# The A11 B11 product of a gated MLP's gate and up as a second Strassen level, with a new order of instructions in a pair's first block

## The chip, the cores and the metric

The kernel runs on one core of one Trainium2 chip. The metric is the device time of one execution in microseconds; a profiled execution also gives the span, from the first to the last instruction of the program.

## The reference, cut to what matters

```python
x = A_x                                              # 1 x 2048 x 640, fp32
g = sigmoid((x * gate_w).sum(-1, keepdims=True))
a = Re(DFT_seq(DFT_hid(x)))                          # einsums with 640x640 and 2048x2048 matrices
b = (gelu(x @ w_gate) * (x @ w_up)) @ w_down         # 640 -> 1728 -> 640
return g * a + (1 - g) * b
```

All arrays are fp32.

## The kernel before, in words

Every fp32 product is made of three fp32r matmuls (`mm3`, L95): an operand is split into `high`, a copy in fp32r by ScalarE, and `low`, the rest, by VectorE; then high x high, high x low and low x high are added up in PSUM. One such triple, 128 x 128 weights on 512 columns, is "a product" here.

The work runs in stages. First, block 0 of the hidden dimension F and the odd 64 columns are computed as plain products. Then comes the loop `for f in range(1, NF)` over 12 blocks of 128 hidden columns (gate and up). After that W_down (`step_k`, 28 steps in `kseq`), then the sequence DFT (`cseq`, 64 steps), then the hidden DFT (`useq`). x and the weights are cut in 2 x 2 block matrices, and all large products use Winograd's form of Strassen's algorithm: seven block products named A11, A12, S1, S2, S3, S4 and A22 in place of eight, with sums T1 to T4 of x's blocks and S1 to S4 of the weights'. Gate is one row of the block matrix and up the other: the first half of the 640 inputs against the second, halves of 1024 rows of x against each other (tp 0 and 1), and a fifth group of 128 inputs by itself (g5, u5 and D).

Blocks 1 and 2 of F are done alone (kind 0). Blocks 3 to 12 are done in five pairs (3,4), (5,6) to (11,12): kind 1 is the pair's first block, kind 2 its second. In a pair, the A12 product of gate (`together`) and the A22 T4 product of up (`together_up`) of both blocks and both halves of x are done with a second Strassen level, 7 products in place of 8. The A11 B11 product isn't: `gate_up` computes it in each block for each half, two products each, and adds the result in PSUM (X) to S2 T2, and from PSUM to the tiles s1 that lead to the gate. The second levels need sums of sums: of x (`xp`, `xv`, made once by `sums_across`, kept in device memory and loaded again in every pair as `xq` and `xu` by `load_across`, three parts of 512 KB each, on POOL's queue), and of weights (`wq` in `make_w`, `wu` in `make_up`).

The order inside a block is written by hand: generators (`gate_up`, `together`, `together_up`) yield after each group of matmuls, and `run` puts ahead of a group's follow-up what `fill` takes from the list `fills`: sums and splits of the next weights, each with a cost in units of 10 ns, paced so that a block's share of fills keeps up with its share of TensorE time. `in_order` fixes the program's order on PE, ACT, DVE and POOL in this stage; SP's loads were ordered by the scheduler of the framework. A tile's buffers come from a pool `s4` of 46 slots of 512 KB, 32 of which x's blocks hold in this stage, and from 14 buffers of 256 KB (`m`): a load waits until its buffer's last reader is done. PSUM has 8 banks.

From the second pair on, the lows of `wa` and `wq` of a first block are not made by VectorE: ScalarE writes the negated high (`negative`), and an accumulating DMA on POOL's queue adds the raw weights (`left_of`).

The gate g is made along the way: `load_z` loads 128 rows of x, one DVE instruction multiplies them with gate_w and sums up (a "z row", 16 in all); `gates` takes the Sigmoid in block 12, `gate_rows` turns the result with a TensorE transpose and stores g and 1 - g, and `gate_tile` loads them spread over all partitions.

Of the kernel before, what the change touches and what calls it, by code (L numbers as in the profile page):

```python
# [15 lines left out]
P = 128  # L16
# [4 lines left out]
NS = S // P  # L21
NP = NS // 2
# [3 lines left out]
XN_AT = [1, 5, 16, 24]  # L26
GM_AT = [2, 15]
EORD = [0, 2, 1, 3, 4]
PAIRED = 3
Z_AT = [5, 10]  # L30
# [4 lines left out]
def kernel(  # L35
# [52 lines left out]
    def negative(lo, raw):  # L88

        nc.scalar.activation(lo, raw, AF.Copy, scale=-1.0)  # L90

    def left_of(lo, raw):

        nc.gpsimd.dma_start(lo, raw, accum_op=ALU.add)

# [23 lines left out]
    ident = pool.tile([P, P], F32, tag="ident", name="ident")  # L119
    z = pool.tile([P, NS], F32, tag="z", name="z")  # L120
# [7 lines left out]
    grd, gmd = (dram.tile([1, S], F32, tag=n, name=n) for n in ("grd", "gmd"))  # L128
# [80 lines left out]
    def load_w(f):  # L209


        if f >= NF:
            return
        ra, rb = slot(F32, [P, 8, P], f"wa{f}r"), wsmall(F32, f"wb{f}")
        nc.sync.dma_start(ra, wf[f - 1, :, :8])
        nc.sync.dma_start(rb, wf[f - 1, :, 8:])
        rq = None
        if pair_of(f) == 1:
            rq = slot(F32, [P, 8, P], f"wq{f}r")
            nc.sync.dma_start(rq[:, 0:2], wf[f, :, 0:2])  # L220
            nc.sync.dma_start(rq[:, 2], wf[f, :, 4])
        wraw[f] = ra, rb, rq

    def load_up(f):

        r = slot(F32, [P, 8, P], f"wu{f}r")
        nc.sync.dma_start(r[:, 0:2], wf[f, :, 2:4])
        nc.sync.dma_start(r[:, 6:8], wf[f - 1, :, 2:4])
        return r

    late_work = []

    def make_up(f, r):

        W, own = {}, {}
# [7 lines left out]
        def high_u():  # L243
            own["u"] = [slot(F32R, [P, 8, P], f"wu{f}{n}") for n in "hl"]
            high(own["u"][0][:, 1:6], r[:, 1:6])
# [8 lines left out]
        return W, [(112, across), (0, high_u), (78, low_u)]  # L254

    def make_w(f):


        ra, rb, rq = wraw.pop(f)
# [17 lines left out]
        def across():  # L277
            tt(rq[:, 3], rq[:, 0], rq[:, 1], op=ALU.add)
            tt(rq[:, 5], ra[:, 0], rq[:, 0], op=ALU.subtract)
            tt(rq[:, 4], rq[:, 3], ra[:, 0], op=ALU.subtract)  # L280

        def across2():
            tt(rq[:, 6], ra[:, 1], rq[:, 4], op=ALU.subtract)
            tt(rq[:, 7], g5, rq[:, 2], op=ALU.subtract)

        def diff():
            d = wsmall(F32R, f"wd{f}")
            tt(rb[:, 1], g5, u5, op=ALU.subtract)
            split(d[:, 0], d[:, 1], rb[:, 1])
            W["D"] = d[:, 0], d[:, 1]  # L290
# [4 lines left out]
        def high_a():  # L295
            if kind == 2:
                v = slot(F32R, [P, 8, P], f"wa{f}")
                own["a"] = v[:, 0:4], v[:, 4:8]
                high(own["a"][0], ra[:, 4:])
            else:  # L300
                own["a"] = parts("wa")
                high(own["a"][0], ra)

        def low_a():
            a = own["a"]
            if kind == 2:
                low(*a, ra[:, 4:])
                W["D"], W["u5"] = at(a, 0), at(a, 3)
                for i in range(2):
                    W["A11", i] = at(a, 1 + i)  # L310
                return
            if kind == 1 and f > PAIRED:
                left_of(a[1], ra)
            else:
                low(*a, ra)
# [3 lines left out]

        def neg_a():  # L320
            negative(own["a"][1], ra)

        def high_q():
            own["q"] = parts("wq")
            high(own["q"][0][:, 1:], rq[:, 1:])

        def neg_q():
            negative(own["q"][1][:, 1:], rq[:, 1:])

        def low_q():  # L330
            q = own["q"]
            if f > PAIRED:
                left_of(q[1][:, 1:], rq[:, 1:])
            else:
                low(q[0][:, 1:], q[1][:, 1:], rq[:, 1:])
            W["A22p"], W["g5n"], W["Dp"] = at(q, 1), at(q, 2), at(q, 7)
            for k in range(4):
                W[f"S{k + 1}p"] = at(q, 3 + k)
# [12 lines left out]
        if kind == 1:  # L351
            if f > PAIRED:
                work = [(0, high_a), (0, neg_a), (84, across), (0, low_a), (56, across2), (0, high_q), (0, neg_q)]
                work += [(84, sums), (0, low_q), (84, sums2), (0, high_c), (56, diff), (122, low_c)]
            else:
                work = [(84, across), (56, across2), (0, high_a), (0, high_q), (122, low_a), (109, low_q)]
                work += [(84, sums), (84, sums2), (56, diff)]
                late_work.extend([(0, high_c), (122, low_c)])
        elif kind == 2:
            work = [(84, sums), (28, diff_here), (0, high_a), (84, sums2), (122, low_a), (61, high_c), (0, low_c)]  # L360
        else:
            work = [(84, sums), (0, high_a), (84, sums2), (0, high_c), (122, low_a), (56, diff), (122, low_c)]
# [49 lines left out]
    def together(f, W, Tp, s1, xs):  # L412


# [7 lines left out]
        mm3(Z, W["S1p"], Tp["T1"], True, False)  # L422
        mm3(Z, W["g5n"], x1[1], False, True)
# [6 lines left out]
        s1[0, 0] = copy(V, f"s1{f}00")  # L430
        yield
        mm3(H, W["S2p"], Tp["T2"], False, True)
# [3 lines left out]
        mm3(H, W["S3p"], Tp["T3"], False, True)  # L436
# [3 lines left out]
        mm3(Z, W["S4p"], Tp["B22"], False, False)  # L440
        mm3(Z, W["Dp"], x1[1], False, True)
        yield 136
        tt(s1[0, 1], s1[0, 1], Z, op=ALU.add)
        tt(s1[0, 1], s1[0, 1], xs[1], op=ALU.add)
        yield
        mm3(H, W["A22p"], Tp["T4"], False, False)
        mm3(H, W["g5n"], x1[0], False, True)
# [37 lines left out]
    def gate_up(f, W, B, tp, s5, s1t, xs, s4):  # L485
# [6 lines left out]
        X, Z = bank(f"pX{n}"), bank(f"pZ{n}")  # L492
        xs[tp] = X
# [7 lines left out]
        prod(X, "A11", (1, 1), True)  # L501
        yield 136
        if not kind:
            V = bank(f"pV{n}")
            nc.scalar.activation(V, X, AF.Copy)
        else:
            s1 = s1t[kind - 1, tp] if (kind, tp) != (1, 1) else None
            if s1 is not None:
                tt(s1, s1, X, op=ALU.add)
        yield  # L510
# [11 lines left out]
        yield  # L522
        prod(X, "S2", "T2", False)
# [3 lines left out]
        mm3(Z, W["D"], x2, False, False)  # L527
        yield 68
        if kind:
            s1 = s1t[kind - 1, tp]  # L530
            nc.scalar.activation(s1, s1, AF.Gelu_apprx_tanh)
        yield
# [7 lines left out]
        nc.scalar.activation(s2, s2, AF.Gelu_apprx_tanh)  # L540
        yield
        if not kind:
# [85 lines left out]
    def gates():  # L628
        nc.scalar.activation(z, z, AF.Sigmoid)
        nc.scalar.activation(table, table, AF.Gelu_apprx_tanh)  # L630

    def gate_rows():

        ps = bank("pgr")
        nc.tensor.transpose(ps[:NS, :P], z, ident)
        g = mtile(F32, "gr")
        nc.scalar.activation(g[:NS, :P], ps[:NS, :P], AF.Copy)
        nc.vector.tensor_scalar(g[:NS, P : 2 * P], g[:NS, :P], -1.0, 1.0, op0=ALU.mult, op1=ALU.add)
        for k, to in enumerate((grd, gmd)):
            nc.gpsimd.dma_start(to.rearrange("o (s p) -> (o s) p", p=P), g[:NS, k * P : (k + 1) * P])  # L640

    def gate_tile(row, tp, name):

        g = pair(F32, name)
        nc.sync.dma_start(g.rearrange("p t c -> p (t c)"), row[:, 2 * tp * T : 2 * (tp + 1) * T].to_broadcast([P, 2 * T]))
# [4 lines left out]
    def load_z(n):  # L650

        r, work = {}, []

        def load():
            sb = zq.pop(0)
            r[0] = sb, slot(F32, [P, D], f"xz{sb}")
            nc.sync.dma_start(r[0][1], xz[sb])
# [270 lines left out]
    make_identity(nc, ident)  # L928
# [91 lines left out]
    Tp, Tu = {}, {}  # L1020

    def sums_across(n, to, blocks, last):
# [19 lines left out]
        def part(k, src):  # L1042
            def do():
                if k == 3:
# [19 lines left out]
    def load_across(f, n, to, kept, k):  # L1064
        v = slot(F32R, [P, 2, T], f"{n}{f}{k}")
        nc.gpsimd.dma_start(v.bitcast(F32), kept[k - 1])
# [4 lines left out]
    def fill(ns):  # L1071

        state["pe"] += ns
        some = False
        while fills and not (some and not fills[0][0]) and state["done"] <= 1.25 * state["all"] * state["pe"] / state["pe_all"]:
            cost, do = fills.popleft()
            do()
            some = True
            state["done"] += cost

    def run(steps):

        ns = next(steps, None)
        if ns is not None:
            fill(ns)
            next(steps)

    s1t, s4 = {}, {}
    Tp.update(B11=at(Bs[0][2, 1], 0), B21=at(Bs[0][2, 1], 1), B22=at(Bs[1][2, 1], 1))
    blocks = [("11", xt[0, 2]), ("12", xt[2, 2]), ("22", xt[2, 3]), ("21", xt[0, 3])]  # L1090
# [3 lines left out]
    with in_order(PE, ACT, DVE, POOL):  # L1094
        for f in range(1, NF):
            kind = pair_of(f)
            if f == PAIRED:
                loadu()
                fills.extend([*t4, *u123[:3], *late_work, *u123[3:], *u4])
            fills.extend(todo)  # L1100
            todo.clear()
            if kind == 1:
                up, work = make_up(f, load_up(f))
                fills.extend(work)
            if kind == 1:
                lw, *w = sum_wd((f - PAIRED) // 2)
                lw[1]()
                fills.extend(w)
            if f == PAIRED - 1:
                loadp()  # L1110
                fills.extend(t123)
            if f == NF - 1:
# [457 lines left out]
```

## Time and profile before

| what | value |
|---|---|
| runs, us | 1022.82, 1023.52, 1023.52; median 1023.52 |
| the profiled execution | 1023.77 us, span 1022.0 us |
| granted TensorE clock | 1.0 |
| HBM | read 186.19 MB, written 68.17 MB, 249 GB/s over the span |
| the loop over f = 1 to 12 | about 46 to 334.5 us of the span |

A row of a timeline gives start and duration in us, engine (PE matmul, PEld weight load, DVE VectorE, ACT ScalarE, POOL GpSimd, SPq a queue of DMA issues), line of the kernel, operation, tiles written and read, shape, and in brackets how long the engine was idle before and what ended that. A row of groups has a count, the busy time, the mean duration in ns and the idle time before. A row of DMAs has the count, the size of one and the median time from issue to landing. Matmul rows overlap, since matmuls are pipelined.

### The profile page before, as it was taken

What the parts mean: (1) busy time and instruction counts of PE and PEld (TensorE: products, weight loads), DVE (VectorE), ACT (ScalarE), POOL (GpSimd) and SP (SyncE); (2) the same over time, 40 slices, a digit from 0 to 9 for tenths busy, and PEclk for the clock granted to TensorE, in tenths of its full rate; (3) what the DMA queues carried; (4) which work ended last, traced back from release to release, by engine and by line L of the source; (5) the groups of instructions that cost most, each with busy time, mean ns of one, the idle gap of its engine ahead of it and who ended that gap; (6) DMA issues with size and microseconds to landing.
All of it is one profiled execution on the core that took longest, in us unless ns stands there. A gap on an engine that the chain in (4) does not pass through costs nothing.

```text
span 1022.0 us, 13215 instructions
## 1 busy us (share of the span) xinstructions
PE 1017.6 (100%) x4510; PEld 842.3 (82%) x4510; DVE 807.8 (79%) x1142; ACT 479.1 (47%) x629; POOL 166.5 (16%) x295
## 2 busy tenths in 40 slices
PE   9999999999999999999999999999999999999998
PEld 7888888888888888888888888888888888888887
DVE  6986878787777978876898975897588859797795
ACT  5544534353535566555455343444344445455440
POOL 0122242323231200100011022102210200021112
PEclk9999999999999999999999999999999999999999
DMA  7445587878798988968766778658866878987856
GB/s 270 168 148 214 194 279 262 290 237 288 222 304 294 406 323 306 314 205 293 276 228 191 248 263 316 213 192 286 310 206 207 296 250 274 327 318 221 268 138 98
DMA packets 92420, 259.19 MB, mean 254 GB/s; under 512 B 12000, under 2 KB 26368, under 8 KB 92352
## 3 DMA queue, kind: packets, MB, share of 16 engines
q1 hardware_dynamic: 66352, 176.85, 51.2%
q0 software_dynamic: 25712, 81.30, 24.4%
q8 instruction: 35, 0.57, 0.2%
q14 instruction: 33, 0.27, 0.1%
q10 hardware_dynamic: 288, 0.20, 0.1%
HBM read 186.19 MB, written 68.17 MB: 249 GB/s over the span
## 4 chain that ended last, share of the span: by engine, by line
PE 94%; issue 3%; DMA 1%; POOL 1%; DVE 0%; POOLq 0%
PE pX L100 6%; PE pX L99 6%; PE pX L98 6%; PE pZ L100 4%; PE pZ L98 4%; PE pZ L99 4%; PE pL L100 3%; PE pL L99 3%; PE pL L98 3%; PE pV L100 2%; PE pV L99 2%; PE pV L98 2%; PE pY L100 1%; PE pY L99 1%; PE pR L100 1%
## 5 line engine op out<-in xcount | busy, mean ns | idle before, releaser
L79 ACT ACTIVATE ch<-csa 128x1024 fp32r<-128x1024 f32 x32 | 34.0, 1064 | 89.3 <-DVE csa L708 66.9
L82 DVE TENSOR_TENSOR cl<-cra,ch 128x1024 fp32r<-128x1024 f32 x32 | 39.1, 1223 | 23.8 <-ACT ch L79 23.6
L79 ACT ACTIVATE ch<-cra 128x1024 fp32r<-128x1024 f32 x32 | 33.9, 1059 | 48.6 <-PE pL L99 18.0
L82 DVE TENSOR_TENSOR cl<-crb,ch 128x1024 fp32r<-128x1024 f32 x32 | 39.1, 1222 | 16.6 <-ACT ch L79 16.6
L99 PE MATMUL pL<-cl,xah 128*128 128x512 f32 x128 | 49.8, 389 | 0.0
L100 PE MATMUL pL<-ch,xal 128*128 128x512 f32 x128 | 49.8, 389 | 0.0
L98 PE MATMUL pL<-ch,xah 128*128 128x512 f32 x128 | 49.3, 389 | 0.0
L79 ACT ACTIVATE ch<-crb 128x1024 fp32r<-128x1024 f32 x32 | 33.8, 1055 | 26.2 <-DVE cl L82 10.4
L388 POOL DMA_DIRECT2D hA<-s x48 | 26.2, 545 | 120.4 <-DVE s L546 100.7
L82 DVE TENSOR_TENSOR cl<-csb,ch 128x1024 fp32r<-128x1024 f32 x32 | 39.2, 1224 | 4.1 <-ACT ch L79 2.3
L82 DVE TENSOR_TENSOR cl<-csa,ch 128x1024 fp32r<-128x1024 f32 x32 | 39.1, 1222 | 3.3 <-PE pR L99 1.7
L82 DVE TENSOR_TENSOR kl<-kw,kh 128x1024 fp32r<-128x1024 f32 (+1 forms) x26 | 31.5, 1211 | 12.7 <-ACT kh L79 12.7
L79 ACT ACTIVATE ch<-csb 128x1024 fp32r<-128x1024 f32 x32 | 34.0, 1062 | 12.4 <-PE pR L100 4.5
L540 ACT ACTIVATE s<-s 128x512 f32<-128x512 f32 x24 | 15.2, 634 | 46.0 <-DVE s L539 46.0
L79 ACT ACTIVATE kh<-kw 128x1024 fp32r<-128x1024 f32 (+1 forms) x26 | 27.1, 1043 | 12.2 <-issue 4.7
L842 POOL DMA_DIRECT2D out<-ks x12 | 6.5, 540 | 158.6 <-DVE ks L841 157.9
L1239 POOL DMA_DIRECT2D uA<-c x8 | 4.3, 540 | 169.8 <-DVE c L1327 169.5
L388 POOL DMA_DIRECT2D hT<-s x48 | 26.0, 541 | 25.3 <-DVE s L563 8.5
L521 ACT ACTIVATE s<-pZ 128x512 f32<-128x512 f32 x24 | 13.8, 597 | 32.9 <-PE pZ L100 26.8
L145 ACT ACTIVATE s<-pX 128x512 f32<-128x512 f32 x40 | 23.2, 597 | 12.4 <-PE pX L100 12.0
L99 PEld LDWEIGHTS pL<-cl,xah 128*128 128x128 f32 x128 | 24.0, 188 | 5.0
L98 PEld LDWEIGHTS pL<-ch,xah 128*128 128x128 f32 x128 | 24.0, 188 | 5.0
(3644 smaller groups left out, 3466.6 us busy)
## 6 DMA issues: line engine op xcount, KB each, us to landing
cra<-in_ct SPq DMA_DIRECT2D x64, 512.0 KB, 4.2
crb<-in_ct SPq DMA_DIRECT2D x64, 512.0 KB, 4.9
hA<-s POOLq DMA_DIRECT2D x48, 256.0 KB, 4.9
hT<-s POOLq DMA_DIRECT2D x48, 256.0 KB, 6.2
kr<-hA SPq DMA_DIRECT2D x24, 512.0 KB, 6.5
kr<-hT SPq DMA_DIRECT2D x24, 512.0 KB, 6.8
ux<-uA SPq DMA_DIRECT2D x24, 512.0 KB, 6.4
ux<-uT SPq DMA_DIRECT2D x16, 512.0 KB, 5.7
```

Source lines behind the costliest of these rows:

```text
L79: nc.scalar.activation(hi, raw, AF.Copy)
L82: nc.vector.tensor_tensor(lo, raw, hi.bitcast(F32), op=ALU.subtract)
L98: nc.tensor.matmul(ps, lh, rh, start=first, stop=False, skip_group_check=True)
L99: nc.tensor.matmul(ps, lh, rl, start=False, stop=False, skip_group_check=True)
L100: nc.tensor.matmul(ps, ll, rh, start=False, stop=last, skip_group_check=True)
L145: nc.scalar.activation(m, src, AF.Copy)
L388: nc.gpsimd.dma_start(to[:, i], src)
L521: nc.scalar.activation(s5, Z, AF.Copy)
L540: nc.scalar.activation(s2, s2, AF.Gelu_apprx_tanh)
L842: nc.gpsimd.dma_start(acc4[:, t] if tp and e == 4 else out[2 * tp + t, e], src)
L1239: nc.gpsimd.dma_start(to[:, i], src)
```

## The change

- A11 B11 of both blocks and both halves becomes a second Strassen level, `together_one`: 7 products in a pair. Its sums of x (`xo`) are made in blocks 1 to 3, kept and loaded again in each pair; its sums of weights (`wo`) are made by `make_two` in the block before. Results: q[0,0] and q[0,1] for the first block, q[1,0] and q[1,1] for the second, where ACT copies them into PSUM ahead of S2 T2 and DVE adds them to s1.
- A pair's first block follows the string `ORDER`, a step per letter: o for `together_one`, t for `together`, u for `together_up`, 1 and 2 for the two halves' `gate_up`. Loads and sums are hung on fixed steps (`XQ_AT`, `XU_AT`, `UP_AT`, `SUMS_AT`, `W1_AT`, `W2_AT`, `Z_AT`). `PAUSE` and `LATER` move the fills inside the block.
- `load_across` issues on SP in place of POOL, and `in_order` takes SP in: its loads and stores follow the order of the code.
- The lows of `wa` and `wq` are made by DVE in all pairs; `negative` and `left_of` go. The gate sums of `wq` (`make_gate`) are made in the first block itself, no longer in the block before.
- The z rows: 10 in the loop over f, 6 in W_down (`ZB_AT`). `gates(0)` in block 12 and `gates(1)` in W_down each store half of g and 1 - g from the partitions as they are; the transpose (`gate_rows`, `ident`) goes. `XN_AT` and `GM_AT` shift two steps.

```diff
+ORDER = "o1ooo2oo1o21tt2tt1tt2tuu1uu2uu1u2"
+PAUSE = 200
+LATER = 1000
+UP_AT = [7, 13]
+SUMS_AT = [14, 19]
+W1_AT = [15, 20]
+W2_AT = 27
+ZB_AT = [7, 8, 10, 11, 12, 13]
+XQ_AT = [5, 9, 11]
+XU_AT = [16, 18, 21]
...
+    def load_gate(f):
+        r = slot(F32, [P, 8, P], f"wq{f}r")
+        for k, src in ((0, wf[f]), (5, wf[f - 1])):
+            nc.sync.dma_start(r[:, k : k + 2], src[:, 0:2])
+            nc.sync.dma_start(r[:, k + 2], src[:, 4])
+        return r
...
+        return Wp, [(84, across), (56, across2), (0, high_q), (109, low_q)]
...
+    def together_one(f, W, Wp, q, xs):
+        H, Z = (bank(f"p{name}{f}o") for name in "HZ")
+        (b11, b21), (_, b22) = ([at(Bs[tp][1, 1], i) for i in range(2)] for tp in range(2))
+        mm3(H, W["A11", 0], b11, True, True)
+        yield 68
+        X = xs[0] = bank(f"pX{f}_0")
+        nc.scalar.activation(X, H, AF.Copy)
+        yield
+        mm3(Z, Wp["S1p"], To["T1"], True, True)
+        yield 68
+        q[1, 1] = copy(Z, f"s0{f}11")
+        yield
+        mm3(X, W["A11", 1], b21, False, True)
+        yield 68
+        q[0, 0] = copy(X, f"s0{f}00")
+        yield
+        mm3(H, Wp["S2p"], To["T2"], False, True)
+        yield 68
+        c = q[0, 1] = copy(H, f"s0{f}01")
+        yield
+        mm3(H, Wp["S3p"], To["T3"], False, True)
+        yield 68
+        tt(q[1, 1], q[1, 1], H, op=ALU.add)
+        yield
+        mm3(Z, Wp["S4p"], b22, False, True)
+        yield 68
+        tt(c, c, Z, op=ALU.add)
+        xs[1] = bank(f"pX{f}_1")
+        nc.scalar.activation(xs[1], c, AF.Copy)
+        yield
+        mm3(H, Wp["A22p"], To["T4"], False, True)
+        yield 68
+        q[1, 0] = copy(H, f"s0{f}10")
+        yield
...
-        prod(X, "A11", (1, 1), True)
-        yield 136
+        if kind == 2:
+            nc.scalar.activation(X, q[1, tp], AF.Copy)
+            s1 = s1t[1, tp]
+            tt(s1, s1, q[1, tp], op=ALU.add)
...
-        nc.gpsimd.dma_start(v.bitcast(F32), kept[k - 1])
+        nc.sync.dma_start(v.bitcast(F32), kept[k - 1])
...
-    with in_order(PE, ACT, DVE, POOL):
+    with in_order(PE, ACT, DVE, POOL, SP):
...
+                for i, name in enumerate(ORDER):
+                    run(steps[name])
+                    if i in XQ_AT:
+                        load_across(f, "xq", Tp, keptp, 1 + XQ_AT.index(i))
+                    if i in XU_AT and f > PAIRED:
+                        load_across(f, "xu", Tu, keptu, 1 + XU_AT.index(i))
+                    if i == UP_AT[0]:
+                        up = make_two(f, "wu", load_two(f, "wu", 2), Wu)
+                    if i == UP_AT[1]:
+                        fills.extend(up)
+                    if i == SUMS_AT[0]:
+                        lw, *w = sums
+                        lw[1]()
+                    if i == SUMS_AT[1]:
+                        fills.extend(w)
...
+                    if before and step >= n - 3:
+                        load_across(f + 1, "xo", To, kepto, step - n + 4)
+                        if step == n - 1:
+                            raws["gate"] = load_gate(f + 1)
```

341 lines of the change are left out of this document (166 added, 175 removed).

## The prediction

> **What bounds the kernel now.** I read the page's busy times first, then the waits of TensorE alone, then TensorE's timeline at the places where it stood still, then the table by stretches. The page says which engine has no room:
>
> ```profile
> span 1022.0 us, 13215 instructions
> ...
> PE 1017.6 (100%) x4510; PEld 842.3 (82%) x4510; DVE 807.8 (79%) x1142; ACT 479.1 (47%) x629; POOL 166.5 (16%) x295
> ...
> PEclk9999999999999999999999999999999999999999
> ```
>
> A busy PE need not be a PE at its peak, so the waits and the starts decide. Here are all waits of PE, and the rows around its one wait in mid-kernel and around the transpose (start, duration, line, tiles):
>
> ```profile
> PE idle L941 <- PEq L1558: 0.8, 1, 0.8
> PE pH11t L98 <- DMA xq<-xp: 0.3, 1, 0.3
> ```
>
> ```profile
> 289.23 0.39 PE L100 MATMUL pV11t<-x05h,wa11l 128*128 128x512 f32 x1
> 289.94 0.50 PE L98 MATMUL pH11t<-xq,wq11h 128*128 128x512 f32 x1 [0.33 <-DMA xq<-xp]
> ...
> 327.33 0.39 PE L100 MATMUL pZ<-x15h,wa 128*128 128x512 f32 x1
> 327.56 0.27 PE L635 MATMUL pgr<-ident,z 128*16 128x128 f32 x1
> 327.59 0.48 PE L98 MATMUL pX<-xT03h,ws12h 128*128 128x512 f32 x1
> 327.90 0.40 PE L99 MATMUL pX<-xT03l,ws12h 128*128 128x512 f32 x1
> ```
>
> Now one pair of blocks by stretches, f=5 and then f=6, with f=1 ahead of it and the start of W_down's second quadrants behind it (columns: stretch and its length, busy time and count on PE, PEld, DVE, ACT, POOL, then the granted clock, the DMA share and GB/s):
>
> ```profile
> 45.90:70.69 24.79, 24.79 (x110) 20.44 (x110) 20.20 (x27) 12.60 (x19) 2.73 (x6) 1.00 0.26 88
> ...
> 142.99:172.99 30.00, 30.00 (x133) 24.77 (x132) 22.73 (x44) 12.42 (x23) 7.21 (x14) 1.00 0.83 291
> 172.99:190.67 17.68, 17.68 (x79) 14.64 (x78) 13.98 (x30) 9.06 (x15) 6.60 (x11) 1.00 0.81 230
> 382.11:420.00 37.89, 37.89 (x169) 31.37 (x168) 29.53 (x30) 25.45 (x28) 2.16 (x4) 1.00 0.87 303
> ```
>
> The code gives the first block of a pair 132 matmuls (26 triples in the two `gate_up`, 11 in `together`, 7 in `together_up`) and the second 78. The pair takes 30.00 + 17.68 = 47.68 us, so 210 matmuls start every 227 ns at a full clock. Nothing else fits between them: the kernel lasts as long as its list of matmuls. What is taken from that list is gained whole, provided that no product has to wait; what the other engines do costs nothing until it is late for a product.
>
> **What leaves the list.** Before, A11 B11 is four triples in each block of a pair (2 halves x 2 depth steps), eight in a pair. Afterwards `together_one` does it in seven. One triple, 3 matmuls, goes in each of five pairs: 15 x 0.227 = 3.4 us. The 227 ns are the measured spacing, not the 0.39 us that a row lasts, since rows overlap. The Trainium skill, "TensorE: Matmul & The Clock Gate", section "Back-to-back issue gap", speaks against the change here: it gives about 131 ns per matmul of 512 columns in a sustained stream, by which the 15 would be worth only an estimated 2.0 us; this trace's 227 ns disagrees, and decides.
>
> The gate's transpose goes too: from 327.33 to the second product of pX at 327.90 are 0.57 us where two spacings are 0.45, so 0.1 us. The one wait, 289.23 to 289.94, is 0.71 where 0.23 is due: 0.5 us. It came from xq, a part streamed through POOL's queue. Those loads move to SP, so this wait has no reason to stay, but five pairs with a third streamed triple of parts have more places for such a one. I let one of the same size stand and count nothing for it. Sum: -3.5 us.
>
> **What is added on the other engines, and its cover.** DVE, in the rows that price it (the first two are neighbours on the timeline and show that a 512-wide sum takes 0.60 us start to start; then groups with count, busy us and mean ns):
>
> ```profile
> 197.11 0.68 DVE L509 TENSOR_TENSOR s<-s,pX 128x512 f32<-128x512 f32 x1
> 197.71 0.68 DVE L569 TENSOR_TENSOR s<-s,s 128x512 f32<-128x512 f32 x1
> ```
>
> ```profile
> 84.68 1.09 DVE L82 TENSOR_TENSOR wq3l<-wq3r,wq3h 128x896 fp32r<-128x896 f32 x1
> ```
>
> ```profile
> L661 DVE CUSTOM_DVE_ANT_0 xz<-xz,gwb 128x640 f32<-128x640 f32 x4 | 3.3, 820 | 2.8 <-DMA hA<-s 2.8
> L82 DVE TENSOR_TENSOR ws9l<-ws9r,ws9h 128x1024 fp32r<-128x1024 f32 x1 | 1.2, 1218 | 0.0
> L82 DVE TENSOR_TENSOR wu7l<-wu7r,wu7h 128x640 fp32r<-128x640 f32 x1 | 0.8, 824 | 1.0 <-DMA hT<-s 1.0
> L278 DVE TENSOR_TENSOR wq9r<-wq9r 128x128 f32<-128x128 f32 x1 | 0.3, 284 | 0.0
> ```
>
> ```profile
> L145 ACT ACTIVATE s<-pX 128x512 f32<-128x512 f32 x40 | 23.2, 597 | 12.4 <-PE pX L100 12.0
> L99 PEld LDWEIGHTS pL<-cl,xah 128*128 128x128 f32 x128 | 24.0, 188 | 5.0
> ```
>
> For a pair from f=5 on: the new weight sums `wo`, 4 x 0.28 + 0.82 = 1.9 us; the lows of `wa` and `wq`, which were a negation on ACT and an accumulating DMA, 1.22 + 1.09 = 2.3; two more 512-wide sums (q[1,1], q[0,1], s1[0,0] for one of A11's), 1.2; one z row less, -0.8. Together +4.6 on 22.73 + 13.98 = 36.7, so 41.3 of the pair's new 207 x 0.227 = 47.0 us, 88%. It fits, if it comes in the right order. I followed DVE's order by these prices through a second block (66 matmuls, 15.0 us): the first block's last sums end about 4 us in, W's sums and lows and the `wo` sums about 13 us in, the block's own last sums about 3 us into the next first block. There the old block's four T sums and two last ones (six x 0.60) end near 6.7 us, before the first new sum on PE's path, q[1,1] += H: H is ready at 7.6 us, the sum ends near 8.3, and together_one's last product writes H at 8.8. Margin 0.5 us. If this cover goes, each pair loses what DVE is late. `wq`'s low is next: two sums by 9.9, its high on ACT by 11.3, its low by 12.4; the product that needs the low starts at 12.7. Margin 0.3 us.
>
> In f=1 the new parts `xo` add four sums and three lows, 7 x 0.60 = 4.2, to 20.20 of 24.79 us: 24.4, nearly full. They go ahead of block 2's weights, whose lows then end near 67 us by my count; block 2 starts at 70.69. No cost. Six z rows (6 x 0.82 us) move into the steps after 382 us, where DVE has 29.53 of 37.89 us: no cost, though their 320 KB loads fall on a DMA share of 0.87. A second Sigmoid there needs ACT, 25.45 of 37.89 us busy; the second half of the gate is loaded three steps (some 5 us each) after it is written, and x's third split two steps later than before, ahead of products that start beyond 520 us: no cost. ACT gets eight copies of 512 columns in a pair and the high of `wo`, and loses a copy and two negations; even with nothing lost, 8 x 0.60 + 0.8 on 12.42 + 9.06 make 27 of 47 us (the row of such a copy is below). GpSimd loses its streamed loads and accumulations and keeps only stores.
>
> **SP's queue, now in the code's order.** A streamed load now stands behind every earlier SP command that waits for a slot or for DVE:
>
> ```profile
> SPq L586 <- DVE dr L579: 53.5, 6, 15.4
> ```
>
> ```profile
> 207.99 0.86 SPq L586 DMA_DIRECT2D wsd<-dr  x2
> ```
>
> ```profile
> xu<-xv POOLq DMA_DIRECT2D x12, 512.0 KB, 5.8
> xq<-xp POOLq DMA_DIRECT2D x10, 512.0 KB, 5.3
> ...
> wa7r<-in_wf SPq DMA_DIRECT2D x1, 512.0 KB, 3.8
> ...
> wa8r<-in_wf SPq DMA_DIRECT2D x1, 512.0 KB, 5.9
> wa9r<-in_wf SPq DMA_DIRECT2D x1, 512.0 KB, 3.9
> ...
> wa11r<-in_wf SPq DMA_DIRECT2D x1, 512.0 KB, 4.5
> ```
>
> The tightest place is up's third part, xu T3, loaded after step 21 of the new order. Ahead of it on SP are the four stores of W_down's sums, which wait for DVE. DVE takes these sums after the two sums of step 19 (ended 20.4 us into the block): stores out by 23.8. The product with T3 is step 28, at 28.6 us. So the load has 4.8 us; behind it wait block f+2's weights and `wo`. Loads of 512 KB that SP issued in this stretch of a pair landed after 3.8, 3.9 and 4.5 us (wa7, wa9, wa11). Bounds: 0 (nothing earlier can be won on a full PE) to 5.9 - 4.8 = 1.1 us in each of four pairs, 4.4 us. I take 0, by the nearest rows. On POOL's queue the same size took a median 5.3 and 5.8 us. The Trainium skill, "DMA: Bandwidth & Descriptors", section "Specifications", gives a first byte 0.4 us sooner on SP's path than on POOL's; the rows point the same way by more, and by the rule alone, an estimated 5.4 us for xu, T3 would be late by 0.6 us in four pairs.
>
> Sum: the profiled execution took 1023.77 us for a span of 1022.0, so 1.77 lie around it. 1023.77 - 3.5 = 1020.3 for such a run; the median of three, 1023.52, is 0.25 lower, so I predict **1020.0 us**.
>
> **Rivals.** (1) Late parts take the gain back: xu T3, or a part of `xo` or xq, lands 0.4 to 1.1 us late in four pairs, as by the 5.3 to 5.9 us rows: 1.6 to 4.4 us, so 1021.6 to 1024.4. For it: the DMA share of 0.83, to which a pair adds three more 512 KB parts. Against it: the accumulating DMAs of wa and wq are gone, and the rows of that stretch are the short ones.
>
> (2) Slower: the gate weights come late. `load_gate` stands last in the second block, behind the third `xo` part; its slot comes free when that block's S sums have been used, about 1.4 us before its end. Then `wq`'s sums, high and low, and the product at 12.7 us. The sums begin at 8.3 us, so issue and landing have 9 us. Three loads of 512 KB that SP, held between them, issued one behind the other would take 3 x 5.9 and end at 16 us, 8 us after the sums' turn, and PE would stand nearly as long; it turns the gain over from 3.5/5 = 0.7 us per pair on. A delay of 2 us in five pairs gives 1020.0 + 10 = 1030. For it: SP's queue once stood 15.4 us on one such wait. Against it: 9 us is well over any landing shown here.
>
> (3) The products that go are worth less than their spacing, if the weight loads, and not the columns, set the pace where they stood: 188 ns each (the PEld row) in place of 227, 15 x 0.188 = 2.8 us, 1020.6. Against it: the spacing is 227 ns everywhere in the pair. The Trainium skill's 131 ns, above, would be this rival in a stronger form; the trace shows it nowhere.
>
> **How the numbers follow.** No change is what lies within 0.2%, 2.05 us, about what a measurement of this kernel can tell: 1021.5 to 1025.6. Forecast (0.64, 1019.0 to 1021.4: below by the wait that I let stand and 0.5 of scatter, above by one more wait in two or three pairs); (3) 0.02, faster as well; (1) 0.17, nearly all inside no change; (2) 0.17, nearly all slower. The range leaves out most of (2) and little below: 1018.8 to 1025.0.
>
> **What would show it.** Right: 16 fewer PE instructions (4494); a pair in 47.0 us; no PE wait over 0.5 us between 95 and 335 us; DVE near 41 us in a pair. Wrong: PE waits on DMA xu or xo (rival 1), on `wq` lows or H with DVE waiting on wq raw (rival 2), or a pair whose 207 matmuls are spaced wider than 227 ns. If the gain stands but the total doesn't, look at the steps after 382 us, where z rows were put.

## The result: 1.0% slower, and the profile after

The changed kernel takes 1033.7 us in the median of four runs (1032.66 to 1035.49), the kernel before 1023.52 us (1022.82 to 1026.49) beside it: ratio 1.0095, 95% interval 1.0076 to 1.0114. Forecast were 1020.0 us, range 1018.8 to 1025.0. The profiled run took 1032.66 us. Of its page, the span, the busy times, the clock, and the shares of the chain that ended last:

```profile
span 1030.9 us, 13396 instructions
...
PE 1018.6 (99%) x4494; PEld 837.3 (81%) x4494; DVE 836.0 (81%) x1199; ACT 499.0 (48%) x671; POOL 149.7 (15%) x269
...
PEclk9999999999999999999999999999999999999999
...
PE 81%; issue 8%; DMA 4%; DVE 4%; POOL 2%; ACT 1%; SPq 0%; POOLq 0%; ACTq 0%; DVEq 0%
```

The 16 instructions are gone at an unchanged clock, so the list of matmuls is shorter as forecast; the span is 8.9 us longer. TensorE now waits. These are its waits (kind of product and line, what ended the wait, us in total, times, longest), where before there was one of 0.3 us in mid-kernel:

```profile
PE pH3t L100 <- DMA xq<-xp: 2.1, 2, 1.3
PE pZ5u L100 <- DMA xu<-xv: 0.9, 1, 0.9
PE pZ9u L100 <- DMA xu<-xv: 0.8, 1, 0.8
...
PE pV L100 <- ACT pV L542: 0.7, 1, 0.7
PE pH5u L100 <- DMA xu<-xv: 0.6, 1, 0.6
PE pH11u L100 <- DMA xu<-xv: 0.5, 1, 0.5
PE pX L100 <- ACT pX L535: 0.5, 1, 0.5
PE pH3u L100 <- ACT s L146: 0.5, 1, 0.5
```

The list shows only waits that the semaphores explain. So I also took the distance from start to start of neighbouring matmuls, less 0.227 us, wherever it is over 0.245; this "standstill" is 1.6 us in the whole kernel before and 13.7 us after. Of the 13.7: xu's first part in f=5, 7 and 9, 2.8 us; xq in f=3, 2.6; xu's third part in four pairs, 2.2; `wq`'s low, 4 x 0.4; pV in f=1, 1.0; pX in f=12, 0.8; pH3u, 0.7; the rest 0.5 or less each. So 12.1 more of standstill, 3.6 less of work (16 x 0.227) and 0.4 of slightly wider spacing make the 8.9.

One pair shows how a part comes late. SyncE's issues in f=5 (the block starts at 147.07), and then the matmuls at the two places:

```profile
165.68 1.67 SPq L1103 DMA_DIRECT2D xu<-xv  x2
170.01 1.24 SPq L629 DMA_DIRECT2D wsd<-dr  x2
...
172.31 0.81 SPq L695 DMA_DIRECT2D xz<-in_xz  x1
173.21 0.41 SPq L1103 DMA_DIRECT2D xu<-xv  x1
```

```profile
171.14 0.39 PE L102 MATMUL pH5u<-xT04h,wa5l 128*128 128x512 f32 x1
172.45 0.47 PE L100 MATMUL pZ5u<-xu,wu5h 128*128 128x512 f32 x1 [0.93 <-DMA xu<-xv]
...
177.11 0.39 PE L102 MATMUL pZ<-x122h,ws5l 128*128 128x512 f32 x1
178.08 0.47 PE L100 MATMUL pH5u<-xu,wu5h 128*128 128x512 f32 x1 [0.58 <-DMA xu<-xv]
```

The first part is issued at 165.68, when the low of `wu5` has been made and its raw slot comes free, and is needed at 171.4; the third stands behind the stores of W_down's sums and a row of z, is issued at 173.21 and needed at 177.3. Both had 4 to 6 us for a load of 512 KB. The third part is not the only thing late there: the product also waits for ScalarE's copy out of its bank, which ended at 177.55 here, 0.4 us before the part landed, and in f=7 at 226.61, after it (226.54). By stretches, the pair's first block and its second (columns as before):

```profile
147.07:181.57 34.50, 32.87 (x143) 26.23 (x141) 26.45 (x54) 15.13 (x27) 5.41 (x10) 1.00 0.87 304
181.57:196.50 14.93, 14.93 (x67) 12.39 (x66) 14.53 (x28) 9.45 (x17) 3.24 (x6) 1.00 0.51 184
```

The DMA share is 0.87 and then 0.51, where it was 0.83 and 0.81: the transfers crowd into the block in which every part has a time to keep, and VectorE is busy 97% of the other.

Pairs in the versions that follow, in us from a pair's first product (of `together` in the old order, of `together_one` in the new) to the next pair's, and the single or median time:

| kernel | f=3 | f=5 | f=7 | f=9 | total |
|---|---|---|---|---|---|
| before | 47.77 | 47.68 | 47.68 | 47.68 | 1023.52 |
| after | 50.51 | 49.46 | 48.65 | 49.00 | 1033.7 |
| e1, new order, parts on GpSimd | 57.01 | 58.03 | 56.15 | 52.77 | 1063.58 |
| e11, old order, parts on SyncE | 47.77 | 55.21 | 49.81 | 51.60 | 1043.56 |
| e8, one slot more | 48.31 | 49.77 | 50.65 | 49.41 | 1031.83 |
| e6, five edits | 49.37 | 49.97 | 49.11 | 48.01 | 1035.48 |
| e12, lighter | 47.85 | 47.71 | 47.71 | 47.92 | 1025.22 |
| e13, lighter, with the edits | 47.39 | 47.29 | 47.30 | 47.31 | 1021.16 |
| e14, all edits | 48.31 | 47.32 | 47.29 | 47.31 | 1022.70 |
| e16, all edits but the slot | 50.76 | 49.45 | 47.85 | 48.31 | 1028.91 |

Versions that wait scatter more than the kernel before: e6 and e9 are the same up to W_down, and these four pairs differ by 2.8 us in sum, 1.6 of it at half clock behind e9's wait at xq in f=3 (last section). So single times within 3 us of each other are not told apart below.

### The profile page after: what moved, and what is told of

It reads as the page before. It is cut to its first block, busy times and chain, and to the rows that moved or that the text cites. A ratio compares the mean times of both kernels' runs of the same rounds, so it can differ in the third digit from the quotient of the medians.

```text
span 1030.9 us, 13396 instructions
## 1 busy us (share of the span) xinstructions
PE 1018.6 (99%) x4494; PEld 837.3 (81%) x4494; DVE 836.0 (81%) x1199; ACT 499.0 (48%) x671; POOL 149.7 (15%) x269
## 4 chain that ended last, share of the span: by engine, by line
PE 81%; issue 8%; DMA 4%; DVE 4%; POOL 2%; ACT 1%; SPq 0%; POOLq 0%; ACTq 0%; DVEq 0%
PE pX L100 5%; PE pX L101 5%; PE pX L102 5%; PE pZ L101 3%; PE pZ L100 3%; PE pZ L102 3%; PE pL L101 3%; PE pL L102 3%; PE pL L100 3%; PE pV L100 2%; PE pV L101 2%; PE pV L102 2%; PE pQ L101 1%; PE pY L102 1%; PE pY L101 1%
## 5 line engine op out<-in xcount | busy, mean ns | idle before, releaser
L382 POOL DMA_DIRECT2D hA<-s x48 | 25.9, 540 | 208.9 <-DVE s L589 189.1
L89 ACT ACTIVATE ch<-crb 128x1024 fp32r<-128x1024 f32 x32 | 33.7, 1055 | 25.1 <-DVE cl L92 11.7
L146 ACT ACTIVATE s<-pX 128x512 f32<-128x512 f32 x45 | 26.3, 593 | 15.8 <-PE pX L102 15.0
L102 PEld LDWEIGHTS pL<-ch,xal 128*128 128x128 f32 x128 | 24.0, 188 | 5.0
L745 DVE TENSOR_TENSOR csa<-cra 128x512 f32<-128x512 f32 x32 | 22.0, 687 | 6.6 <-PE pL L101 5.0
```

The source lines that it names most:

```text
L89: nc.scalar.activation(hi, raw, AF.Copy)
L102: nc.tensor.matmul(ps, ll, rh, start=False, stop=last, skip_group_check=True)
L146: nc.scalar.activation(m, src, AF.Copy)
L382: nc.gpsimd.dma_start(to[:, i], src)
L745: tt(s1[:, 0], r1[:, 1], r1[:, 0], op=ALU.subtract)
```

## The experiments

The kernel before took 1023.61 us beside e1 to e8, 1022.94 beside e9 to e11, 1026.97 beside e12 to e14, and 1024.51 (median) beside e15 to e17.

**Order and queue, one at a time.** First the new order with the streamed parts on GpSimd's queue again:

```diff
-        nc.sync.dma_start(v.bitcast(F32), kept[k - 1])
+        nc.gpsimd.dma_start(v.bitcast(F32), kept[k - 1])
```

> The changed kernel, with the streamed parts xo, xq and xu issued by POOL again and all else as in the change. In the changed kernel's trace TensorE stands 2.6 us for xq in the first pair, 2.8 us for xu T1 and 2.1 us for xu T3: 7.6 us. Theory buffers (a part's load waits for a slot whose last reader or store is done): POOL waits for the same slots, so at least 5 of the 7.6 us stay, or more come, since POOL has the block's stores in its queue; span 1029 to 1034. Rival queue (the load is held by SP commands ahead of it that wait for something else): most of the 7.6 us go, span about 1024 to 1026.

1063.58 us, and the waits of TensorE:

```profile
PE pH3t L100 <- DMA xq<-xp: 4.2, 1, 4.2
PE pH11o L100 <- DMA xo<-xo: 4.0, 1, 4.0
PE pH5o L100 <- DMA xo<-xo: 4.0, 1, 4.0
...
PE pH5u L100 <- ACT s L146: 3.2, 1, 3.2
```

After their issue the parts land about as before (xq 5.8, xu 4.9, xo 4.3 us in the median, against 6.6, 5.6 and 3.4 on SyncE); they are issued later, behind stores on the same queue that wait for finished sums. The wait at pH5u (and one of 3.1 us at pH7u) is of another kind: xu's third part had landed 3 us before, and TensorE waits for ScalarE's copy out of the bank, which stands behind the split of the next block's weights. GpSimd's longest group of waits between 95 and 335 us:

```profile
POOL hA L382 <- DVE s L589: 72.0, 8, 21.4
```

Standstill 44.8 us, of which 10.9 are not waits but matmuls at half clock behind them (last section). So the move to SyncE saves this order some 30 us in all; it doesn't cost it 10.

The other part alone, the kernel before with its parts on SyncE (the same line the other way round):

> The kernel before with one part of the change alone: its streamed parts xq and xu are loaded by SyncE in place of GpSimd, at the same places of the code. Theory (the stalls come from the new order of a pair's first block, in which each part has little time between its slot coming free and its product, not from the loading engine): 1023.6 us within 2 us, pairs 47.7 us as before. Rival (SyncE's queue itself makes parts late: a part waits behind other loads and stores there): the same waits at xq and xu T1 and T3 as in the changed kernel, over 1 us in each pair, total above 1028.

1043.56 us: neither. The old order loses 20 us to the queue, but not at the parts. VectorE's waits, its row at the longest, and TensorE's:

```profile
DVE xz L661 <- issue: 9.7, 1, 9.7
DVE xz L661 <- DMA xz<-in_xz: 8.0, 1, 8.0
```

```profile
160.56 0.82 DVE L661 CUSTOM_DVE_ANT_0 xz<-xz,gwb 128x640 f32<-128x640 f32 x1 [9.74 <-issue]
```

```profile
PE pH5t L98 <- DVE s L438: 5.2, 1, 5.2
```

Rows of z, now behind the parts in one queue, land (between 130 and 220 us) after a median of 11.1 us where it was 5.5; VectorE, whose order is fixed, stands at such a row, and the sum that TensorE needs (L438) stands behind it. Of the 20 us, 5.6 are matmuls at half clock behind these waits. So order and queue fit each other; either alone is worse than both.

Next, SyncE out of the fixed order:

```diff
-    with in_order(PE, ACT, DVE, POOL, SP):
+    with in_order(PE, ACT, DVE, POOL):
```

> The changed kernel, with SP left out of the fixed order (the framework orders SP's loads itself, as before the change). Theory buffers: waits for xq and xu stay within 2.5 us of the 7.6 us, span 1028 to 1034. Rival queue: xu T3 (2.1 us), which stands behind the four stores of W_down's sums, and part of xu T1 and xq go; 4 us or more less, span below 1027.

1032.72 us, and the standstill is 13.73 us to the changed kernel's 13.74. Only its places are others: f=3's xq wait is gone, and now

```profile
PE pH5u L100 <- ACT s L146: 1.7, 1, 1.7
PE pH7u L100 <- ACT s L146: 1.6, 1, 1.6
```

At these two, xu's third part had landed 1.5 and 1.3 us before; they wait for ScalarE's copy, as in e1. The loss is not due to the written order of SyncE.

**One wait at a time.** `PAUSE` holds the fills back at the start of a pair; less of it should make `wq`'s low earlier. Another version loads xu's third part ahead of W_down's sums and z's row. A third adds a slot of 512 KB for one buffer of 256 KB:

```diff
-PAUSE = 200
+PAUSE = 150
```

> The changed kernel with PAUSE = 150 in place of 200, so that the second half of the gate sums and the high of wq come a step earlier. In the changed kernel TensorE stands 0.40 us in each of four pairs at the first product with wq's low. Theory chain (sums, high on ACT, low on DVE end 0.4 us too late): these four waits of 0.4 us go, nothing else changes by more than 0.5 us; span 1028.8 to 1030. Rival (the low is late because the raw wq lands late): they stay.

```diff
-SUMS_AT = [14, 19]
+SUMS_AT = [18, 22]
...
-Z_AT = [(4, 9), (11, 15), (20, 28)]
+Z_AT = [(4, 9), (11, 15), (22, 28)]
```

> The changed kernel with two orders on SP changed: SUMS_AT = [18, 22] in place of [14, 19], so that W_down's weights are loaded after xu T2 and their sums' four stores stand behind xu T3, and the third z row is loaded after xu T3 too. Theory queue, for xu T3 alone: T3 is issued some 2 us earlier (in the changed kernel 26 us into the first block, right behind the stores, which wait for DVE), its waits of 2.1 us in all go, and xu T1, with nothing of W_down's ahead of it, gains too (2.8 us before): span 1026 to 1028. Rival buffers: T3 waits for a slot just as long, its waits stay within 0.7 us, span 1030 to 1031.5.

```diff
-        return pool.tile(shape, dt, tag="s4", name=name, bufs=46)
+        return pool.tile(shape, dt, tag="s4", name=name, bufs=47)
...
-        return pool.tile([P, T], dt, tag="m", name=name, bufs=14)
+        return pool.tile([P, T], dt, tag="m", name=name, bufs=13)
```

> The changed kernel with 47 slots of 512 KB in place of 46, and 13 small buffers in place of 14. Theory buffers: a load that waited for a slot is issued one release earlier, so the waits for xq in the first pair (2.6 us) and for xu (4.9 us) fall by half or more; span 1025 to 1027.5, unless the missing small buffer makes waits of its own at copies of ACT. Rivals queue and bandwidth: they stay within 1.5 us, span 1029.5 to 1032.

Each took its wait away, and none the time. 1036.46 us without the four waits for `wq`'s low: xu's third part now stands 2.8 us in f=5. 1037.21 us without a wait for xu: in f=5 and f=7 the product of `together_up` with T14 (T4 of x's second half) waits 1.5 us for a sum of VectorE, and a product of W_down 2.4 us (the stage takes 5.8 us longer). 1031.83 us with the slot: xq in f=3 is on time, and xu's third part is 1.8 and 2.1 us late in f=5 and f=7.

**Less traffic.** Two versions with a stream left out: e3 reads resident tiles in place of the parts xo (other data), e7 neither loads nor sums the z rows of the loop over f (a gate of 0.5 in their place):

```diff
-                        load_across(f + 1, "xo", To, kepto, step - n + 4)
+                        To[f"T{step - n + 4}"] = at(Bs[0][1, 1], (step - n) % 2)
```

> The changed kernel without the reloads of xo: the products of together_one read resident tiles of x in place of the sums, so their data are other ones, and 1.5 MB and three slots per pair are not used. Rival bandwidth (three more parts of 512 KB in a pair make all parts land later): median landing of xu and xq falls by 1 us or more below 5.6 and 6.6 us, and the 7.6 us of waits fall to 3 or less. Theory buffers: the slots that xu waits for late in the first block are others, xu's 4.9 us of waits stay within 1.5 us; the first pair's xq may gain. Span 1028 to 1032 by buffers, below 1027 by bandwidth.

```diff
+    nc.vector.memset(z, 0.5)
...
-                pieces = load_z(3 if f < PAIRED + 6 else 2) if f > PAIRED else []
+                pieces = []
```

> The changed kernel without the ten z rows in the loop over f (the gate is then not the reference's): two or three loads of 320 KB, a slot and 0.8 us of DVE for each go from every first block from f=5 on. Theory crowding (in the changed kernel the DMA share is 0.87 in a first block and 0.51 in a second): xu and xq land earlier, and their waits after the first pair (4.9 us) fall by half or more; span 1026 to 1028.5. Rival queue/chain: waits stay within 1.2 us, span 1029.5 to 1031.

1031.39 and 1028.0 us. The parts' loads between 95 and 335 us of the changed kernel, of e3 and of e7 (size, median us from issue to landing):

```profile
xq<-xp SPq DMA_DIRECT2D x15, 512.0 KB, 6.6
...
xu<-xv SPq DMA_DIRECT2D x12, 512.0 KB, 5.6
```

```profile
xq<-xp SPq DMA_DIRECT2D x14, 512.0 KB, 3.9
xu<-xv SPq DMA_DIRECT2D x12, 512.0 KB, 4.5
```

```profile
xu<-xv SPq DMA_DIRECT2D x12, 512.0 KB, 4.7
```

With fewer transfers beside them the same loads land up to 2.7 us sooner, xq in e7 alone hardly (6.5). So the crowding is real, but one stream is not all of it. Both left out:

> The changed kernel without two of its streams at once: the parts xo are read from tiles that are resident (other data), and the rows of z are not loaded and summed (the gates come from a constant), so 12 parts of 512 KB and 11 rows of 320 KB... fewer go through the pairs; SyncE still loads xq and xu in the order written. Theory (every wait is a part that is late because slots, SyncE's order and the crowded DMA each take from the same few us): the waits at xq and at xu T1 and T3 fall below 1 us in sum over a pair, and what is left is 1.0 us at pV of f=1, 0.4 us at wq low in four pairs and 0.8 us in f=12; 1023 to 1026 us. Rival (SyncE's waits for VectorE's slots alone make them late): the waits stay near 2 us per pair, total above 1029.

1025.22 us, with 6.4 us of standstill: all waits for parts together 0.5 us in f=9 and less elsewhere; pV, `wq`'s low and pX of f=12 as listed. And with the edits that take those away:

> The same two streams left out of the kernel of e9_xn_later, whose edits took the waits at pV, wq low and f=12 away. Theory (the shorter product list is worth its 3.5 us once every part is on time): 1019.5 to 1022 us, below the kernel before, pairs 47.0 to 47.5 us. Rival (the new order costs something of its own, beside the late parts): above 1024 us with waits that name neither a DMA nor a load.

1021.16 us, pairs of 47.3 us, 2.7 us of standstill. The one run of the kernel before beside it, 1026.97, is 3.5 us above its first median; against that median, 1023.52, the gain is 2.4 us. No wait for a part is left, and the loss of the change is gone. What is left in each pair is 0.27 us at the product with T14, which waits for VectorE's sum out of the same bank. The two streams take slots, queue, transfers and, with the z rows, VectorE's time with them, so these two runs show that they make the loss together, not which of these does.

**The whole kernel, edited.** Five edits together: `PAUSE` and the sums as above, `UP_AT = [7, 11]`, the high of T2 moved from the end of the first stage into block 1's fills, and the gates of block 12 after its second step:

```diff
-                gates(0)
-                nc.scalar.activation(table, table, AF.Gelu_apprx_tanh)
...
+                    if f == NF - 1 and step == 1:
+                        gates(0)
+                        nc.scalar.activation(table, table, AF.Gelu_apprx_tanh)
```

> e5 plus four edits, one for each other wait: PAUSE = 150 (wq's low, 1.6 us in all), UP_AT = [7, 11] (the low of wu, which frees xu T1's slot, two steps earlier), gates(0) two steps later in block 12 (the two table loads ahead of the copy that X waits for, 0.77 us), and the high of x's T2 behind the first copy of block 1 (1.0 us). If the waits are separate causes, all of these go and 2.5 us in the first pair stay: span 1021 to 1024. If the pair's first block is bound by what its loads and its DVE work take in all, waits that are removed come back at the next part: span 1026 or more.

1035.48 us: pV, `wq` and xu wait no more, but W_down takes 178.4 us where it took 169.55. Six matmuls of block 12 now stand in this stage and wait there (2.3 us together), and 2.5 us are matmuls at half clock (last section); the rest is a wait. The wait of TensorE there, and ScalarE's row ahead of it:

```profile
PE kX L100 <- ACT kb0040h L89: 3.8, 1, 3.8
```

```profile
364.50 0.85 ACT L89 ACTIVATE xah<-xn 128x768 fp32r<-128x768 f32 x1 [7.18 <-DMA xn<-in_xn]
```

ScalarE, in a fixed order, stands 7.2 us at rows of x that are needed after 520 us, and the split of the next weights stands behind it. Loading these rows later (`XN_AT = [5, 10, 18, 24]`):

> The five edits of the run before them and one more: in the W_down stage the first two loads of x's natural rows (`load_xn`) come at steps 5 and 10 in place of 1 and 5. Theory (many chains, each with its own cover): the W_down stage of the five-edit kernel was 178.4 us instead of 169.55 only because the 640 KB of xn sat 11 us behind other transfers and held ACT for 7.2 us; with them later the stage is back within 1 us of 169.6 and the total is 1035.5 - 8 = 1027 us or a little less, below the changed kernel's 1033.7 and still above 1023.5, since the pair part (242.3 us) and f=3's xq waits are as they were. Rival (the stage is short of DMA bandwidth whatever comes first): another load is late in its place, stage above 173 us, total above 1030.

That wait is gone, as expected, and the stage takes 172.2 us: 169.55, the six matmuls of block 12, and their wait. The total, 1032.39 us, is not the 1027 expected: beside these 2.7 us the four pairs took 2.8 us more than in e6, a scatter of the kind named above. With two rows of z in each of the later pairs and eight in W_down (`load_z(2)`, `ZB_AT` longer), and `XN_AT = [4, 6, 18, 24]` (the changed kernel has 3, 3, 2 and 2 rows there, so two rows move):

> As e9_xn_later (xn at steps 4 and 6), and two rows of z in each of the four later pairs in place of 3, 3, 3, 2, the three left over in the W_down stage. Theory (the waits for DVE in f=5 and f=7, 1.75 us each at T14, come from VectorE's third row total of 2.3 us in the pair's second block): these two waits go, 3.5 us, and the total is 1023 to 1025 us if the W_down stage takes three more rows at no cost. Rival: T14 waits stay above 1 us (the queue order, not the row total), total 1026 to 1028; or W_down pays for its rows.

1036.46 us: the T14 waits shrank to 0.6 us, and W_down paid 6.9 us at one product, and 1.8 at half clock behind it. Then the edits of e10 with `XN_AT = [5, 10, 18, 24]`, `ZB_AT` from step 8, `GM_AT = [2, 18]` and 47 slots:

> Nothing left out: the edits of e10_xn_later_even_rows with the loads of xn at steps 5 and 10 and z's rows from step 8 on, and 47 slots with 13 small ones. Theory: e10's pairs without f=3's wait at xq (1.5 us) and without the W_down stage's stall of 8.4 us: 1036.5 - 10 = 1026.5 us, 1024 to 1029. Rival (a saturated DMA moves the wait each time): a new wait of over 3 us somewhere between 335 and 400 us, total above 1030.

> The kernel of e14_all_edits again, timed against the kernel before in five rounds. Theory (the shorter list of products is worth about 3.5 us, less 1.1 us left in f=12 and 0.5 us in f=3): 1021.5 to 1024 us, ratio 0.996 to 1.000, and pairs near 47.3 us. Rival (e14's single time was a lucky run of a kernel whose transfers are on the edge): above 1026 us in the median.

1022.70 us, and timed in five rounds 1022.89 us (1022.43 to 1024.32) to 1024.51 before (1023.14 to 1032.16): ratio 0.998, interval 0.9966 to 0.9995. So the mended kernel is faster, by no more than the 0.2% that the prediction calls no change. Waits of TensorE in e14, and its f=5 and f=6 by stretches:

```profile
PE pX L100 <- DVE s L573: 0.8, 1, 0.8
...
PE pH3u L100 <- DVE s L506: 0.3, 1, 0.3
```

```profile
143.20:176.20 33.00, 33.00 (x145) 26.85 (x145) 26.57 (x54) 15.86 (x29) 5.98 (x11) 1.00 0.82 279
176.20:190.60 14.40, 14.40 (x66) 11.89 (x65) 13.73 (x26) 8.78 (x16) 2.71 (x5) 1.00 0.78 265
```

The transfers are spread over both blocks again, and PE is busy throughout both. Which edit kept the parts ahead? The same without the slot, and the same with three rows of z in f=5 and f=7 again:

> e14's kernel with 46 slots and 14 small ones again. Theory (the extra slot gives f=3's xq its time, and the later pairs have theirs from the other edits): xq in f=3 waits 1.5 to 3 us again, pairs from f=5 on stay under 48 us, total 1024 to 1027 us. Rival (the slot is what keeps all parts ahead): waits at xq or xu in every pair, total above 1029.

> e14's kernel with 3, 3, 3 and 2 rows of z in the four later pairs, as in the changed kernel, and six in the W_down stage. Theory (a row more is 2.3 us of VectorE in the second block, where VectorE is busy 97% of the time, and 320 KB beside the parts): T14's wait comes back at 1.0 to 1.75 us in f=5, f=7 and f=9, total 1026 to 1029 us. Rival (the row costs nothing once a slot is free): within 1 us of e14_all_edits.

Without the slot 1028.91 us, with standstills at xq in f=3 (3.4 us) and at the products of `together` in f=5 and f=9, between the two expectations. With more rows 1022.79 us: with the slot the rows cost nothing, and my reading of the T14 waits as the third row's was wrong. Without the slot the rows are not cleared: e16, with two, stands 0.5 us at T14 in f=5 and f=7, e9, with three, 1.6. SyncE's issues for f=7, without the slot (the block starts at 195.2) and with it (190.6):

```profile
180.43 13.05 SPq L1102 DMA_DIRECT2D xo<-xo  x3
...
198.81 0.33 SPq L1102 DMA_DIRECT2D xq<-xp  x1
...
204.74 4.95 SPq L1102 DMA_DIRECT2D xq<-xp  x2
```

```profile
175.55 10.21 SPq L1102 DMA_DIRECT2D xo<-xo  x3
...
190.83 0.38 SPq L1102 DMA_DIRECT2D xq<-xp  x1
...
198.24 2.41 SPq L1102 DMA_DIRECT2D xq<-xp  x2
```

Measured from the block's start, xq's first part is issued 3.6 us into it without the slot and 0.2 with it, the second 9.5 and 7.6. One slot lets the whole queue behind it run ahead. Alone, in e8, it did not help: there each place that it freed met the next late operand.

## Why the prediction was wrong

**The list of matmuls** held: 4494 instructions, still 227 ns apart where none waits. Not all of its 3.5 us reaches the time: the later pairs of e13 and e14 take 47.3 us, not the 47.0 forecast, so 0.38 us of 0.68 is gained in each; 0.27 stands at the product with T14.

**DVE's cover** held in size and mostly in order: 26.45 + 14.53 = 41.0 us in the pair, 41.3 forecast, and q[1,1] += H was never late. The next margin failed: `wq`'s low, given 0.3 us, was late by 0.4 us in four pairs, 1.6 us. A margin of 0.3 us at the end of a chain of sums, a high and a low is no margin.

**f=1, "no cost"**: VectorE's count was right, but the 1.0 us came from ScalarE, whose copy into pV stands behind the highs of T2 and two copies of block 0. I had priced the engine that was full, not the one whose order had changed.

**SP's queue** is the step that failed in full. I took the tightest part, xu's third, at 0 with a bound of 4.4 us for four pairs; it cost 2.2. The stores of W_down's sums ended 25.1 us into the block (f=5) and not 23.8, a row of z stood behind them in f=5 and f=7 that I had not counted, and the load went out at 25.9 to 26.4 us. It landed 3.8 to 4.7 us later, much as I had taken it: the start was wrong, not the landing. The Trainium skill's sooner first byte on SP's path, which I had weighed here ("DMA: Bandwidth & Descriptors", "Specifications"), cannot be seen in the landing times, among other transfers: xq and xu landed 6.6 and 5.6 us after their issue, on POOL's queue before 5.3 and 5.8. And the parts that I put at nothing cost more: xu's first, 2.8 us, and xq in f=3, 2.6 us. xu's first was issued when `wu`'s raw slot came free and then took 6.1 to 6.9 us in f=5, 7 and 9, where I had 3.8 to 4.5 for the third; xq in f=3 was held until a slot came free. "The tightest" was found by order in the queue alone; what a load's slot waits for was never followed. SyncE's waits in that stretch say which:

```profile
SPq L1103 <- DVE wd L92: 38.4, 4, 9.8
SPq L1103 <- DMA hT<-s: 28.9, 7, 8.5
SPq L629 <- DVE dr L622: 15.9, 6, 4.9
```

Two waits for slots at the line of the parts (L1103) are both longer than the wait for W_down's sums (L629), the only one that I had reckoned with. The first is the second part of the next pair's xo, in the second block (9.3 to 9.8 us each time), the second is xq: 8.5 us in f=3, and 6.7 us ahead of its third part in f=5, 7 and 9, until stores of finished results (hT) had landed. Whatever stands behind them on SyncE starts late too.

**Block 12's gates, "no cost"**: `gates(0)` and the table back to Gelu put two table loads ahead of the copy into pX, in ScalarE's order, and the product waits 0.8 us:

```profile
328.62 1.28 ACT L675 ACT_TABLE_LOAD   x1
...
330.14 1.28 ACT L1172 ACT_TABLE_LOAD   x1
...
331.55 0.58 ACT L535 ACTIVATE pX<-s 128x512 f32<-128x512 f32 x1
```

**The steps after 382 us** were right: the stage takes 169.55 us in both kernels. That they are nearer the edge than they look, the edited versions show.

**The rivals.** (2), the late gate weights, did not come, and (3), products worth less than their spacing, neither. (1), late parts, was the mechanism, mis-sized: 0.4 to 1.1 us in four pairs, 4.4 at most, against 7.6 us at parts alone and 12.1 in all. I had bounded one part at a time with the landing times of a spread-out stream. In the new order three more parts share the slots, the queue and the first block's bandwidth with the others, and a late one moves the rest. e2 and e5 (the queue) and e8 (the slots) show that freeing one of these changes which operand is late and hardly how much; with less traffic, e7's standstill fell by 4.4 us and e3's by 1.1. How the loss splits among the three is not shown.

What stays open: how the gain splits among the edits of e14. The slot is worth 6 us with the others there (e16) and about nothing without them (e8); the others were not taken back one by one.

## What to carry to other kernels

Where a full engine is fed by streamed operands, a change that adds streams is priced by following each load back through three things at once: the command ahead of it in its queue, the last reader of its buffer, and what else is in flight when it goes out. If removing one wait leaves the total as it was, stop mending single waits and look for what all late operands share; here a single buffer more, after the local edits, turned a loss of 0.4% into a gain of 0.2%. Try the parts of a change one at a time before blaming one: here each half alone was worse than both.

## What the runs showed of the hardware

A long wait of TensorE costs more than itself. In e11, PE stood 5.2 us until 162.04; the stretches around it (the clock is the third number from the end):

```profile
156.00:162.00 6.00, 0.80 (x4) 0.34 (x2) 1.44 (x4) 0.00 (x0) 0.00 (x0) 0.97 0.98 362
162.00:164.00 2.00, 1.96 (x5) 1.57 (x6) 1.93 (x6) 0.99 (x2) 0.00 (x0) 0.50 0.02 8
...
166.00:168.00 2.00, 2.00 (x10) 1.64 (x9) 1.97 (x6) 0.78 (x2) 0.00 (x0) 1.00 0.91 264
```

The granted clock is 0.50 for 3.41 us from 161.58 on and 1.00 after that. The eight matmuls after the wait start within 3.30 us where 1.82 are due, so the wait cost 1.5 us more. Such stretches of 3.41 or 6.83 us stand behind waits in seven of the versions, with matmuls 0.43 us apart; beside the waits they cost 10.9 us in e1, 5.6 in e11, 2.5 in e6, 2.0 in e5, 1.8 in e10 and 1.6 each in e3 and e9. The kernels before and after and the other versions have none in mid-run.

The wait need not be so long. In e11 a wait of 2.0 us that ended at 263.24 had such a stretch behind it:

```profile
264.00:267.30 3.30, 3.30 (x9) 2.58 (x8) 3.20 (x7) 2.32 (x4) 0.00 (x0) 0.50 0.50 158
```

After e16's longest wait, 2.75 us, the clock stayed at 1.00 and the spacing was 0.23 to 0.31 us at once. The traces show what sets the two apart. In each, all changes of the clock lie whole steps of 3.41 us apart, so I added up the standstill in each step. In 13 of the 14 cases in which the clock fell, TensorE had stood for 2.1 us or more in the step before; after steps at full clock with 1.8 us or less it never fell; close to 2.05 us it fell once and once not. e11's short wait put 2.2 us into one step; e16's was split into 1.6 and 1.35. The Trainium skill, "TensorE: Matmul & The Clock Gate", Part 1, says that the clock falls to half after an idle window of about 3.4 us and comes back after as long a busy one. The step agrees with it; but 2.1 us of standstill in a step were enough here.
